# Queue order in the late attention heads: stores and loads first on SP, splits and output products behind the next head's scores and turns

## The chip, the cores and the metric

The program runs on one core of a Trainium2 chip. The metric is device time in microseconds (us). The engines are TensorE (matmuls; PE in the profile, its weight loads PEld), VectorE (DVE), ScalarE (ACT), GpSimd (POOL) and SyncE (SP), which here only issues transfers (DMAs). Each engine works through its own queue in order.

## The reference

For 4 × 8 = 32 heads of 576 positions and 64 columns, decayed causal attention; then two feed-forward layers over the 2304 tokens:

```
cum    = cumsum(log(clip(f, 1e-4, 1)))
scores = q k^T / 8 + cum[i] - cum[j], masked above the diagonal
attn   = exp(scores - max) / (sum + 1e-9);  o = attn v
x      = o, heads side by side: 2304 x 512
x      = relu(x w_in)^2 w_out            # first layer, 512 -> 2048 -> 512
h      = x w_in';  out = (h - tanh(h)) w_out'   # second layer, same sizes
```

## The kernel before, in words

Matmuls run on float32r operands; a product of full precision is made of three, with each operand split into a rounded part and the rest (`rounded` and `rest`, lines 93 to 106 by engine). So nearly each tile has a rounding and a subtraction behind it.

The main loop at the end of the function walks over feed-forward blocks: 8 of the first layer (288 tokens each), then 5 of the second. A block has 16 steps; step i issues 12 matmuls of the first product (`h_step`, line 143), and, two steps later, 12 of the second (`y_step`, line 169). Between these half steps the attention is advanced by pieces (`advance`): a generator `chain` gives one piece at each `yield`. Tokens 0 to 575 belong to heads 0 to 7 and so on, so blocks wait for x from the attention; x goes through DRAM (`store_x`, `load_x`).

Heads 0 to 15 turn the probabilities by TensorE. Heads 16 to 31 (`UT` = 16 on), the late ones, do it through DRAM, and the change is about them. For a late head k the steps are:

- `load(k)` (lines 228 to 232): q and k into R (one buffer), and decay rows into QB (two buffers); `load_v(k)` (line 250) into VR (two buffers). All transfers are issued by SP.
- `prep(k)`: R is rounded to QA on ScalarE; VectorE makes QA's rest, GpSimd QB's rounding (line 95) and QB's rest (line 106).
- `scores(k, t)` for tiles t = 4, 3, 2, 1, 0 of query rows, 576, 448, 320, 192 and 64 keys wide: two matmuls (lines 490, 491), a row minimum on VectorE (451) into the P tile T, the exponential on ScalarE (456), and a normalisation (465) by VectorE for t = 4, 2, 0 and by GpSimd for t = 3 and 1. The P tiles are two, used in turn.
- `turn(k, t)`: VectorE transposes the 32 × 32 blocks in place (517).
- `put_get(k)`: five stores of T to DRAM (526, 527: the "put") and six loads that bring it back rearranged (532, 534: the "get").
- `split_p(k, a)`, a = 0 for chunks 0 and 1, a = 1 for 2 and 3: per chunk a rounding on GpSimd into PTh (95) and a rest on VectorE into PTl (106). PTh and PTl have one buffer each.
- `prep_v(k)`: V rounded on ScalarE, its rest on GpSimd; `pv(k)` (570 to 576): the output products of PTh, PTl and V, and the copies into xs; every second head `store_x`.

In `attention_late` the body for k scores head k and finishes head k − 1, in five pieces. The order that is written is not the order of issue. The program is built twice: up to the start of block 2 (`MARK`) the written order is forced on each engine; after it a planner at build time issues, by its own estimate of when inputs are there, the earliest written of the instructions that are ready. `tc.issue_after(x)` adds, for each instruction of the block on x's engine, that it is queued behind x, without a wait for x to finish; `latest(engine)` is the last instruction written so far on that engine. Feed-forward steps carry such ties to earlier attention pieces (`SLK`).

Of the kernel before, what the change touches and what calls it, by code (L numbers as in the profile page):

```python
# [18 lines left out]
NU = B * H  # L19
# [14 lines left out]
UT = 16  # L34
# [24 lines left out]
def kernel(  # L59
# [25 lines left out]
    def pre(u):  # L85
        return "" if u < UT else "l_"

    def by(name):
        return {"A": nc.scalar, "V": nc.vector, "P": nc.gpsimd, "S": nc.sync}[ENG[name]]

    def rounded(eng, out, in_):
        if eng is nc.scalar:
            eng.activation(out, in_, AF.Copy)  # L93
        elif eng is nc.gpsimd:
            eng.tensor_scalar(out, in_, 1.0, 1.0, ALU.mult, ALU.mult)  # L95
        else:
            eng.tensor_copy(out, in_)
# [7 lines left out]
    def rest(eng, out, in_, hi):  # L105
        eng.tensor_tensor(out, in_, hi.bitcast(F32), ALU.subtract)  # L106
# [76 lines left out]
    def latest(engine):  # L183
        return next(x for x in reversed(nc.cur_bb.bb.instructions) if x.engine == engine)
# [43 lines left out]
    def load(u):  # L228
        R[u] = one.tile([128, 2, S], F32, tag="R", name="R")
        nc.sync.dma_start(R[u], qk[u])  # L230
        QB[u] = two.tile([68, 2, S], F32R, tag="QB", name="QB")
        nc.sync.dma_start(QB[u][64:68].bitcast(F32), aug_d[u])
# [7 lines left out]
    def prep(u):  # L240
        r = R.pop(u)
        qa = two.tile([128, 2, S], F32R, tag="QA", name="QA")
        QA[u] = qa
        split_qk(r, qa, QB[u], *(pre(u) + x for x in ("qb_q", "qa_lo", "qb_lo")))
        ST[u] = two.tile([128, 4, 6], F32, tag="ST", name="ST")
        by(pre(u) + "st").memset(ST[u], 1.0)

    def load_v(u):
        VR[u] = two.tile([128, 5, D], F32, tag="VR", bufs=2, name="VR")
        nc.sync.dma_start(VR[u], v[u])  # L250
# [216 lines left out]
    def bank(u, name):  # L467
        return psa.tile([128, 512], F32, tag="at", name=name)

    def blocks(u):  # L470
        return PT[u % 2].rearrange("p (k s j) -> p k s j", s=4, j=32)
# [3 lines left out]
    def prob(u, t, a, b):  # L475
        rows = 64 if t == 0 else 128
        if u < UT:
            return P[t][:rows, a:b]
        k0, sl = (16, 2) if t == 0 else (0, t - 1)
        return blocks(u)[:rows, k0 + a // 32:k0 + b // 32, sl]  # L480
# [34 lines left out]
    def turn(u, t):  # L515
        x = prob(u, t, 0, NKEY[t])
        nc.vector.transpose(x, x)  # L517
# [5 lines left out]
    def put_get(u):  # L523
        T, (d, e) = PT[u % 2], p_d[u % 2]
        for q in range(4):
            by("put").dma_start(d.rearrange("(i q) n -> q i n", q=4)[q], T[32 * q:32 * q + 32, :2048])  # L526
        by("put").dma_start(e, T[:, 2048:])
        src = d.rearrange("(i q) (a b n) -> b i (q a) n", q=4, a=4, b=4)
        end = e.rearrange("(q i) (b s n) -> b i q s n", q=4, b=2, s=2)
        for b in range(4):  # L530
            dst = T[32 * b:32 * b + 32]
            by("get").dma_start(dst[:, :2048].rearrange("p (q n) -> p q n", q=16), src[b])  # L532
            if b < 2:
                by("get").dma_start(dst[:, 2048:].rearrange("p (q n) -> p q n", q=4), end[b][:, :, 1])  # L534

    def split_p(u, a):
        src = PT[u % 2][:, :2048].rearrange("p (q a s j) -> p q a s j", q=4, a=4, s=4)
        for c in (2 * a, 2 * a + 1):
            s0 = max(0, c - 1)
            hi, lo = (late_pt(k)[:, :, CHUNK_AT[c]:CHUNK_AT[c] + 4 - s0] for k in "hl")  # L540
            rounded(by("pth"), hi, src[:, :, c, s0:])
            rest(by(f"ptl{c}"), lo, src[:, :, c, s0:], hi)

    def late_pt(k):
        return PT[k].rearrange("p c j -> p (c j)")[:, :1664].rearrange("p (q c j) -> p q c j", q=4, j=32)

    def pv(u):
        vh, vr = VH.pop(u), VR.pop(u)
        b, h = divmod(u, H)
        e = h % 2  # L550
        ps = bank(u, "o_ps")
        if u < UT:
            hi, lo = (PT[k] for k in "hl")
            po = ps.rearrange("p (s j) -> p s j", s=4)
            at = lambda p, c, t: p[:, 10 - 4 * c + t:14 - 4 * c]
            po4, p4 = ps[0:64, 384:512].rearrange("p (q j) -> p q j", q=4), blocks(0)[0:64, 12:16, 1]
            po_at = lambda t: po[:, t:]
            p0 = blocks(0)[0:64, 8:10, 0]
        else:
            hi, lo = (late_pt(k) for k in "hl")  # L560
            po = ps.rearrange("p (q s j) -> p q s j", q=4, s=4)
            at = lambda p, c, t: p[:, :, CHUNK_AT[c]:CHUNK_AT[c] + 4 - t]
            end = PT[u % 2][0:64, 2048:].rearrange("p (q s j) -> p q s j", q=4, s=2)
            po4, p4 = po[0:64, :, 3], end[:, :, 1]
            po_at = lambda t: po[:, :, t:]
            p0 = end[:, 0:2, 0]
        seq = [(hi, 0), (None, 4), (None, 0), (hi, 1), (lo, 1), (hi, 2), (lo, 2), (hi, 3), (lo, 3), (lo, 0)]
        for n, (pt, c) in enumerate(seq):
            if c == 4:
                nc.tensor.matmul(po4, vr[0:64, 4], p4, start=False, stop=False)  # L570
            elif pt is None:
                ps0 = bank(u, "o0_ps")
                nc.tensor.matmul(ps0[0:64, 0:64], vr[0:64, 0], p0, start=True, stop=True)
            else:
                t = max(0, c - 1)
                nc.tensor.matmul(po_at(t), vh[:, c].rearrange("p a d -> p (a d)"), at(pt, c, t), start=(n == 0), stop=(n == 9))  # L576
        if e == 0:
            XS[0] = two.tile([128, S], F32, tag="xs", name="xs")
        xs = XS[0]
        r = slice(64 * e, 64 * e + 64)  # L580
        xt = one.tile([64, 512], F32, tag="xsh", name="xt")
        rounded(nc.scalar, xt, ps[64:128])
        if u < UT:
            nc.vector.tensor_tensor(xs[r, 64:], ps[0:64], xt, ALU.add)
        else:
            nc.vector.tensor_tensor(
                xs[r, 64:].rearrange("p (s q j) -> p q s j", s=4, q=4),
                ps[0:64].rearrange("p (q s j) -> p q s j", q=4, s=4),
                xt.rearrange("p (q s j) -> p q s j", q=4, s=4), ALU.add,
            )  # L590
        rounded(by(pre(u) + "xs0"), xs[r, 0:64], ps0[0:64, 0:64])
        if e == 1:
            store_x(b, h // 2, xs, 0, S)
# [11 lines left out]
    def attention(u0):  # L605
        for p in range(u0 - 2, UT):
            if u0 - 1 <= p:
                load_v(p + 1)
            for t in (1, 4, 3, 2):
                if p >= u0:  # L610
                    trans(p, t)
                    yield
                if u0 <= p + 1:
                    scores(p + 1, t)
                    if t == 1:
                        scores(p + 1, 0)
                    elif p + 1 == UT:
                        turn(UT, t)
                    yield
                if t == 4 and p + 2 < NU:  # L620
                    prep(p + 2)
                if t == 3 and p >= u0:
                    prep_v(p)
            if p + 3 < NU:
                load(p + 3)
            if p >= u0:
                pv(p)
            if p + 1 == UT:
                turn(UT, 1)
                turn(UT, 0)  # L630
                put_get(UT)
            if p >= u0:
                yield

    def attention_late():
        for k in range(UT + 1, NU + 1):
            now = k < NU
            if now:
                load_v(k)
                clear(k)  # L640
                scores(k, 4)
            yield
            if now:
                scores(k, 3)
                turn(k, 4)
            yield
            if k + 1 < NU:
                prep(k + 1)
            prep_v(k - 1)
            split_p(k - 1, 0)  # L650
            if now:
                scores(k, 2)
                turn(k, 3)
            yield
            if k + 2 < NU:
                load(k + 2)
            split_p(k - 1, 1)
            if now:
                scores(k, 1)
                scores(k, 0)  # L660
                turn(k, 2)
            yield
            if now:
                turn(k, 1)
                turn(k, 0)
                put_get(k)
            pv(k - 1)
            yield

    X = {0: [f1.tile([128, NK, TB], F32R, tag="xhl", bufs=4, name="xhl") for _ in range(2)]}  # L670
# [223 lines left out]
```

## Time and profile before

| | |
|---|---|
| median of 3 runs (lowest, highest) | 1102.18 us (1101.27, 1104.58) |
| profiled execution: its time, its span | 1104.67 us, 1102.8 us |
| TensorE busy over the span | 1032.4 us (94%) |
| VectorE, ScalarE, GpSimd busy | 585.9, 526.7, 255.0 us |
| chain that ended last | PE 51%, DMA 9%, DVE 4%, SP's queue 4% |
| transfers | 137.99 MB, mean 125 GB/s |

Busy time is summed over stages with different limits; idle time of an engine that is not the limit costs nothing. The late heads run from about 255 to 585 us. In a row "[7.45 <-POOL PTh L95]" says that the engine stood idle for 7.45 us before, and what ended it. The name of a tile stands without its buffer number, so heads are told apart by order: a head's stores (line 526) come once, the first of head 16's at 256.68 us.

### The profile page before, as it was taken

The page shows a single profiled execution, that of the slowest core. Times are in us where ns is not written, and L with a number is a line of the kernel's source. Part 1 is how long each engine was busy: PE and PEld are TensorE (multiplying, and loading weights), DVE is VectorE, ACT ScalarE, POOL GpSimd, SP SyncE. Part 2 cuts the span into 40 slices and gives each one's busy share as a digit, 9 for nine tenths or more (in the row PEclk, how much of TensorE's full clock was granted, in tenths as well). Part 3 has the DMA queues.
Part 4 walks back from the last instruction along what each step waited for, and adds up shares of the span by engine and source line. Part 5 has one row for each costly group of instructions (what it writes and reads, how often), then busy time and mean ns, then how long its engine had stood idle before and what let it go on. Part 6 is the DMA issues. An engine that isn't in the chain of part 4 may idle for free.

```text
span 1102.8 us, 17026 instructions
## 1 busy us (share of the span) xinstructions
PE 1032.4 (94%) x6048; PEld 909.0 (82%) x6048; DVE 585.9 (53%) x1550; ACT 526.7 (48%) x1221; POOL 255.0 (23%) x374
## 2 busy tenths in 40 slices
PE   4899999998989789989799999999999999999998
PEld 3576779887978688879789999888888888888898
DVE  5886777776677666957533545644222222222222
ACT  6977777764554454645435757532222222222222
POOL 4244455555345353533310000000000000000000
PEclk9989999998998898999899999999999999999999
DMA  7556643228766758766738149300300200110010
GB/s 243 193 148 196 183 154 121 79 79 234 213 172 181 208 146 257 222 145 176 197 84 328 53 143 345 133 1 1 115 1 1 88 27 1 39 39 1 1 39 20
DMA packets 95558, 137.99 MB, mean 125 GB/s; under 512 B 12048, under 2 KB 72016, under 8 KB 93424
## 3 DMA queue, kind: packets, MB, share of 16 engines
q1 hardware_dynamic: 95472, 136.89, 41.4%
q8 instruction: 48, 0.79, 0.3%
q14 instruction: 38, 0.31, 0.1%
HBM read 94.99 MB, written 41.88 MB: 124 GB/s over the span
## 4 chain that ended last, share of the span: by engine, by line
PE 51%; DMA 9%; DVE 4%; SPq 4%; POOL 1%; issue 1%; ACT 1%; POOLq 0%; ACTq 0%; DVEq 0%
PE yp L169 25%; PE hp L143 24%; DMA p_d<-T 4%; DMA T<-p_d 3%; DVE PTl L106 1%; SPq L532 1%; SPq L526 1%; PE o_ps L576 1%; SPq L534 1%; POOL PTh L95 1%; DMA xhl<-x_d 1%; DMA raw<-in_w_dram 1%; DVE T L517 1%; DVE gl L106 1%; DVE T L465 0%
## 5 line engine op out<-in xcount | busy, mean ns | idle before, releaser
L143 PE MATMUL hp<-xhl,w 128*128 128x288 f32 (+2 forms) x2496 | 457.5, 331 | 6.7 <-ACT tmp L153 4.0
L143 PEld LDWEIGHTS hp<-xhl,w 128*128 128x128 f32 x2496 | 394.6, 194 | 45.5 <-ACT tmp L153 5.2
L169 PE MATMUL yp<-ghl,w 128*128 128x512 f32 (+1 forms) x960 | 214.9, 373 | 0.0
L169 PE MATMUL yp<-gh,w 128*128 128x288 f32 x1024 | 199.3, 301 | 0.0
L169 PEld LDWEIGHTS yp<-ghl,w 128*128 128x128 f32 x960 | 167.8, 188 | 34.2
L169 PEld LDWEIGHTS yp<-gh,w 128*128 128x128 f32 x1024 | 161.6, 192 | 1.6 <-issue 0.4
L158 DVE TENSOR_TENSOR tmp<-hp,tmp 128x512 f32<-128x512 f32 (+1 forms) x80 | 51.0, 638 | 208.2 <-ACT tmp L157 208.1
L157 ACT ACTIVATE tmp<-hp 128x512 f32<-128x512 f32 (+1 forms) x80 | 44.5, 556 | 223.2 <-PE hp L143 223.1
L169 PE MATMUL yp<-gl,w 128*128 128x288 f32 x512 | 132.7, 303 | 4.6 <-DVE gl L106 3.7
L153 ACT ACTIVATE tmp<-hp 128x288 f32<-128x288 f32 x128 | 51.7, 405 | 123.3 <-PE hp L143 121.7
L456 ACT ACTIVATE T<-T,ST 128x320 f32<-128x320 f32 (+4 forms) x152 | 82.8, 546 | 45.8 <-DVE ST L451 39.4
L169 PEld LDWEIGHTS yp<-gl,w 128*128 128x128 f32 x512 | 91.0, 193 | 7.2 <-DVE gl L106 5.1
L106 DVE TENSOR_TENSOR gl<-tmp,gh 128x288 fp32r<-128x288 f32 x96 | 47.8, 499 | 64.5 <-ACT tmp L155 63.9
L106 DVE TENSOR_TENSOR PTl<-T,PTh 128x512 fp32r<-128x512 f32 (+1 forms) x64 | 53.0, 857 | 50.0 <-POOL PTh L95 49.0
L106 DVE TENSOR_TENSOR ghl<-tmp,ghl 128x512 fp32r<-128x512 f32 (+1 forms) x80 | 51.1, 639 | 49.1 <-ACT ghl L93 43.8
L451 DVE CUSTOM_DVE_ANT_0 T<-s_ps,mk 128x320 f32<-128x320 f32 (+3 forms) x152 | 61.8, 421 | 21.4 <-PE s_ps L491 13.2
L465 POOL TENSOR_SCALAR T<-T,ST 128x448 f32<-128x448 f32 (+4 forms) x80 | 52.4, 657 | 89.6 <-DVE ST L460 43.3
L93 ACT ACTIVATE ghl<-tmp 128x512 fp32r<-128x512 f32 (+1 forms) x80 | 47.2, 590 | 49.9 <-DVE tmp L158 49.8
L576 PE MATMUL o_ps<-PTh,VH 128*128 128x512 f32 (+1 forms) x96 | 40.4, 421 | 29.3 <-POOL PTh L95 25.4
L95 POOL TENSOR_SCALAR PTh<-T 128x512 fp32r<-128x512 f32 (+1 forms) x64 | 43.9, 710 | 73.3 <-DMA T<-p_d 72.8
L106 DVE TENSOR_TENSOR w<-wst,w 128x512 fp32r<-128x512 f32 x64 | 45.8, 722 | 25.8 <-ACT w L93 25.6
L154 ACT ACTIVATE gh<-tmp 128x288 fp32r<-128x288 f32 x128 | 56.6, 443 | 4.4 <-PE yp L169 1.3
(119 smaller groups left out, 1217.3 us busy)
## 6 DMA issues: line engine op xcount, KB each, us to landing
raw<-in_w_dram SPq DMA_DIRECT2D x64, 512.0 KB
p_d<-T SPq DMA_DIRECT2D x64, 256.0 KB
T<-p_d SPq DMA_DIRECT2D x64, 256.0 KB
R<-in_qk_dram SPq DMA_DIRECT2D x24, 576.0 KB
xhl<-y_d SPq DMA_DIRECT2D x16, 512.0 KB
xhl<-x_d SPq DMA_DIRECT2D x14, 576.0 KB
y_d<-yst SPq DMA_DIRECT2D x14, 576.0 KB
VR<-in_v_dram SPq DMA_DIRECT2D x32, 160.0 KB
```

The costliest lines, as they stand in the source:

```text
L93: eng.activation(out, in_, AF.Copy)
L95: eng.tensor_scalar(out, in_, 1.0, 1.0, ALU.mult, ALU.mult)
L106: eng.tensor_tensor(out, in_, hi.bitcast(F32), ALU.subtract)
L143: nc.tensor.matmul(ps, w[:, k * 128:(k + 1) * 128], xk, start=(jj == 0), stop=(jj == 11))
L153: nc.scalar.activation(tmp, ps, AF.Relu)
L154: nc.scalar.activation(gh, tmp, AF.Square)
L158: nc.vector.tensor_tensor(tmp, ps, tmp, ALU.subtract)
L169: nc.tensor.matmul(yp[m][:, :n], w[:, c], x, start=(i == 0 and j == 0), stop=(i == NF - 1 and j == 2))
L451: nc.vector.tensor_tensor_reduce(out, s_in, m_in, -0.125, 3.0e38 if mn is None else mn, ALU.add, ALU.min, accum_out=acc)
L456: nc.scalar.activation(p, p, AF.Exp, bias=mn, scale=-1.0, accum_out=st[:rows, 1, t:t + 1])
L465: by(n_by).tensor_scalar(p, p, st[:rows, 3, t:t + 1], 1.0, ALU.mult, ALU.mult)
L576: nc.tensor.matmul(po_at(t), vh[:, c].rearrange("p a d -> p (a d)"), at(pt, c, t), start=(n == 0), stop=(n == 9))
```

## The change

`split_p(k - 1, 0)` is written behind `scores(k, 2)` and `turn(k, 3)` and tied behind the latest instruction of VectorE and of GpSimd; `split_p(k - 1, 1)` behind the scores of tiles 1 and 0 and `turn(k, 2)` and tied behind VectorE's latest. `pv(k - 1)` is tied behind TensorE's latest. The loads of V for k + 1 and of q, k and decay for k + 2 move to the end of the body, behind `put_get(k)` and `pv(k - 1)`, tied behind SP's latest. For head 18 `load` moves in the same way from `attention`.

```diff
@@ attention
-            if p + 3 < NU:
+            if p + 3 < NU and p + 1 < UT:
                 load(p + 3)
...
                 put_get(UT)
+                loads(UT)
             if p >= u0:
                 yield
+
+    def loads(k):
+
+        with tc.issue_after(latest(EngineType.SP)):
+            if k + 1 < NU:
+                load_v(k + 1)
+            if k + 2 < NU:
+                load(k + 2)
@@ attention_late
             if now:
-                load_v(k)
                 clear(k)
                 scores(k, 4)
...
             prep_v(k - 1)
-            split_p(k - 1, 0)
             if now:
                 scores(k, 2)
                 turn(k, 3)
+            with tc.issue_after(latest(EngineType.DVE)), tc.issue_after(latest(EngineType.Pool)):
+                split_p(k - 1, 0)
             yield
-            if k + 2 < NU:
-                load(k + 2)
-            split_p(k - 1, 1)
             if now:
                 scores(k, 1)
                 scores(k, 0)
                 turn(k, 2)
+            with tc.issue_after(latest(EngineType.DVE)):
+                split_p(k - 1, 1)
             yield
             if now:
                 turn(k, 1)
                 turn(k, 0)
                 put_get(k)
-            pv(k - 1)
+            with tc.issue_after(latest(EngineType.PE)):
+                pv(k - 1)
+            loads(k)
             yield
```

## Rows read from the trace of the kernel before

**Rows 1.** Windows: us, busy PE, PEld, DVE, ACT, POOL; PE clock, DMA share, GB/s.

```profile
255.00:585.00 330.00, 290.09 (x1898) 274.41 (x1897) 212.13 (x632) 160.22 (x407) 128.49 (x173) 0.91 0.69 187
...
695.00:1102.00 407.00, 403.93 (x1945) 337.07 (x1943) 127.32 (x206) 109.33 (x193) 0.00 (x0) 1.00 0.08 29
```

**Rows 2.** Waits of TensorE, 255 to 600 us: total, times, longest.

```profile
PE o_ps L576 <- POOL PTh L95: 25.4, 8, 7.4
```

**Rows 3.** Timeline of TensorE: start, duration, engine, line, operation, tiles, [idle before].

```profile
359.76 0.28 PE L491 MATMUL s_ps<-QB 68*128 68x64 f32 x1
...
369.96 0.80 PE L576 MATMUL o_ps<-PTh,VH 128*128 128x512 f32 x1 [7.45 <-POOL PTh L95]
```

**Rows 4.** Timeline of SP's queue: start and duration of issue.

```profile
296.15 2.69 SPq L526 DMA_DIRECT2D p_d<-T  x4
...
354.78 3.44 SPq L526 DMA_DIRECT2D p_d<-T  x4
...
364.50 1.22 SPq L532 DMA_DIRECT2D T<-p_d  x2
...
376.86 2.82 SPq L526 DMA_DIRECT2D p_d<-T  x4
...
388.57 2.99 SPq L526 DMA_DIRECT2D p_d<-T  x4
...
392.40 1.31 SPq L230 DMA_DIRECT2D R<-in_qk_dram  x1
...
475.87 1.18 SPq L230 DMA_DIRECT2D R<-in_qk_dram  x1
...
555.01 3.38 SPq L526 DMA_DIRECT2D p_d<-T  x4
```

**Rows 5.** Chain that ended last, in order of time: start, duration, what.

```profile
364.50 3.78 DMA T<-p_d
...
398.32 5.14 DMA T<-p_d
...
451.69 3.56 DMA R<-in_qk_dram
...
462.13 8.95 DMA xhl<-x_d
```

**Rows 6.** Timeline of ScalarE, heads 24 (QA) and 22 (T).

```profile
360.12 1.18 ACT L93 ACTIVATE QA<-R 128x1152 fp32r<-128x1152 f32 x1
...
361.72 0.47 ACT L456 ACTIVATE T<-T,ST 128x192 f32<-128x192 f32 x1
```

**Rows 7.** Timeline of GpSimd.

```profile
291.44 2.31 POOL L95 TENSOR_SCALAR PTh<-T 128x512 fp32r<-128x512 f32 x4
...
369.29 2.91 POOL L95 TENSOR_SCALAR PTh<-T 128x512 fp32r<-128x512 f32 x4 [9.43 <-DMA T<-p_d]
372.18 0.66 POOL L95 TENSOR_SCALAR QB<-QA 64x576 fp32r<-64x576 f32 x1
372.81 1.70 POOL L106 TENSOR_TENSOR QB<-R,QA 64x576 fp32r<-64x576 f32 x1
...
375.10 0.69 POOL L465 TENSOR_SCALAR T<-T,ST 128x192 f32<-128x192 f32 x1
...
545.60 2.49 POOL L95 TENSOR_SCALAR PTh<-T 128x512 fp32r<-128x512 f32 x4 [0.52 <-DMA T<-p_d]
```

**Rows 8.** Timeline of VectorE.

```profile
369.94 1.09 DVE L106 TENSOR_TENSOR PTl<-T,PTh 128x512 fp32r<-128x512 f32 x1 [6.64 <-POOL PTh L95]
...
375.51 0.47 DVE L451 CUSTOM_DVE_ANT_0 T<-s_ps,mk 128x320 f32<-128x320 f32 x1
...
376.08 0.88 DVE L517 STREAM_TRANSPOSE T<-T 128x192 f32<-128x192 f32 x3
...
412.09 1.36 DVE L465 TENSOR_SCALAR T<-T,ST 128x320 f32<-128x320 f32 x1
...
422.06 0.39 DVE L465 TENSOR_SCALAR T<-T,ST 128x320 f32<-128x320 f32 x1
```

## The prediction

> **What bounds the kernel now.** I read the windows first, then who waits for whom, then the timelines of one pair of heads. From 255 to 585 us, where the sixteen late heads run, TensorE is busy 290.09 of 330.00 us at a mean granted clock of 0.91, so it stands idle for 39.9 us; from 695 us on it is busy 403.93 of 407.00 [rows 1]. The change touches only the first of these stretches. There 25.4 us of TensorE's waiting, in 8 pieces, is an output product that waits for the rounding on GpSimd [rows 2]. One piece: head 22's last score starts at 359.76, head 21's first output product at 369.96 after 7.45 us of nothing [rows 3].
>
> TensorE is not what sets the pace, since it waits. A loop of latencies does: scores, turns, store ("put"), load back ("get"), rounding and split of one head, and only then scores again in the same one of two P tiles. Head 18's store starts at 296.15 and head 31's at 555.01, thirteen steps later [rows 4]: 258.86 / 13 = 19.91 us a head, 39.8 us for two, which is one pass of the loop.
>
> Head 21 shows its parts. Its store starts at 354.78 [rows 4]; its last loads are issued at 364.50 and landed 3.78 later, at 368.28 [rows 5]: a round trip of 13.5 us. GpSimd rounds it from 369.29 after 9.43 us of idleness [rows 7], VectorE splits from 369.94 after 6.64 [rows 8].
>
> Both engines work in order, and there lies the loss. Head 22's exponential for tile 1 starts on ScalarE at 361.72 and lasts 0.47 [rows 6], so it is done at 362.19. Its normalisation runs on GpSimd at 375.10, because head 21's four roundings (2.91) and then the rounding and rest of QB for head 24 (0.66 and 1.70) stand ahead [rows 7]. Its turns run at 376.08 [rows 8], its store at 376.86 [rows 4], 22.1 us after head 21's. For head 23 the normalisation happened to stand ahead of head 22's rounding, and its store follows after 11.7 us, at 388.57 [rows 4]. In nine of the fourteen heads 18 to 31 the rounding of the head before stands ahead of the last normalisation; the first such rounding is at 291.44, the last at 545.60 [rows 7].
>
> A pass without such a block is head 21 to 23: 388.57 − 354.78 = 33.8 us. Against the mean of 39.8 that is 6.0 us; over the 6.5 passes of the thirteen steps 39 us. This is the most that the change can give, and about TensorE's idle time.
>
> **The change part by part.** The profiled execution took 1104.67 us, 1.87 of it around its span of 1102.8, and 2.49 above the median of the runs, 1102.18. I work out a difference and take it off the median.
>
> *Split behind turns.* Nothing is added or removed: per head four roundings, four rests and ten products are put behind other instructions of their engines. The first half (chunks 0 and 1) may no longer precede turn 3 on VectorE, the second not turn 2; on GpSimd the first half is tied only behind the rest of V. So the normalisation of tile 1 and the last two turns are not tied ahead of anything; the second half merely comes after the scores of tile 1 in the written order, so a planner that takes the earlier written of two ready instructions lets that normalisation pass. In head 22: two roundings (1.46), then the normalisation (0.69) ends at 369.29 + 1.46 + 0.69 = 371.44, and after the first two rests the turn gives a store at about 373, 4 us sooner. If all four roundings stay ahead, only head 24's QB is gone from the queue (its data now come later, below): the last turns then stand behind the four rests on VectorE, which end just ahead of the row minimum at 375.51 [rows 8], so the store comes at about 375.5, 1.4 us sooner. If the normalisation passes all four, the store comes at about 364, some 12 us sooner. I take 4, the middle case, because the tie on GpSimd is the weak one. A pass has one store, and 9 in 14 of the stores are blocked: 4 × 9/14 × 6.5 = 17 us less; bounds 6 and 39 (the 50 of the best case is more than there is).
>
> *The tie costs something.* The second half now waits for turn 2, and the P tile comes free later by one turn, 0.88 / 3 = 0.3 us [rows 8]: 0.3 × 6.5 = 2 us more; bounds 0 and 4 (two turns). Hidden elsewhere it is not, since the tile's release is in the loop.
>
> *VectorE beside GpSimd.* More normalisations on VectorE will run beside GpSimd's work. The row shows what that can cost: 320 columns took 1.36 us at 412.09, in front of which VectorE had been free, and 0.39 at 422.06 [rows 8]. About 1.0 us in 9 of 14 heads is up to 4 us; I take 1, since the roundings that used to stand beside the rests now stand beside turns. The Trainium skill, "SBUF — State Buffer", section "SBUF: two separate sides", says that the two engines lock one pair of ports for a whole instruction and the loser stands still. By that rule every such meeting would cost the whole of GpSimd's instruction, and the term would be the full 4; the two rows agree with the lock, but not every meeting in the trace is that dear.
>
> *Loads behind the round trip.* Loads of q and k (R, QB) and of V are now queued on SP behind the head's gets (and, for odd heads' outputs, behind the stores of x). Head 26's load of R at 392.40 stood between head 23's store at 388.57 and its gets [rows 4], whose last was issued at 398.32 and landed 5.14 later [rows 5]: a round trip of 14.9 against 13.5. Two of the fourteen heads had it so, the other with R at 475.87 [rows 4]. Each gives 1.4 us to one of the two interleaved chains of passes, half to the end: 2 × 1.4 / 2 = 1 us less; bounds 0 and 5 (if R just ahead of a store did the same in half of the heads, 7 × 1.4 / 2).
>
> The price is that R comes a head or more later. After head 21's gets are issued (364.50 + 1.22) head 23's R would be issued at about 366.5 and land after 3.56 us, as one did [rows 5], at 370.1, or that much after the gets' landing, at 371.8. ScalarE's rounding of q and k takes 1.18 [rows 6], GpSimd's two QB steps 2.36 behind the four roundings, which end at 372.2 [rows 7]: 374.6 to 375.4, then the score product. Head 23's first row minimum is at 375.51 now, held by the P tile [rows 8]. So the new path ends where the old one ends: I take 0. But nothing is left in reserve. A large transfer ahead of R takes 8.95 where x was loaded [rows 5]: the upper bound is 8.95 − 3.56 = 5.4 us a pass, 35 in all; below, 0.
>
> *Output products behind TensorE's latest.* Head 21's product already stood ten us behind the last score, with feed-forward matmuls between [rows 3]. I take 0; bounds −3 and +3 for one group of feed-forward matmuls to either side.
>
> *The start.* Head 18's loads go behind head 16's gets, beside the load of x for the next block: 0, bounds 0 and 3.
>
> Sum: −17 + 2 + 1 − 1 = −15 us: 1104.67 would become about 1090, and the median 1102.18 − 15 = 1087 us. TensorE's idle time should fall from 39.9 to about 25 us; matmuls at the lower clock behind each stall get fewer, but that is inside the loop's time and not counted again.
>
> **The rivals.** *Clean passes.* All normalisations get ahead; the loop runs at 33.8 a pass: 39 less, 1063 us. For: head 23 shows that it happens. Against: the ties don't reach the normalisation of tile 1.
>
> *No change.* The planner puts all four roundings ahead as now, and the 6 us that the lower bounds leave are eaten by the tie and the start: 1102, within 3. For: the last two turns, for which the store waits, are untied.
>
> *Slower: R becomes the last to release the scores.* Place: the first score of head k+2 behind QB, behind R, behind the gets on SP. Price: if R lands 5.4 us later than reckoned in five of the passes, +27, less the 15 gained: +12, 1114 us. It decides the sign once R's path is longer than the P tile's by 15 / 6.5 = 2.3 us a pass. For: no reserve, and DMA share 0.69 in this stretch [rows 1]. Against: a head's gets end before R starts, so usually little is in front of it.
>
> **How the numbers follow.** Forecast (1072 to 1097) 0.42, clean passes 0.14, no change 0.14, R late 0.30. The range that leaves 2 in 10 out reaches into both sides: 1062 to 1118. What a measurement can tell from no change is 0.3%, 3.3 us. Faster: 0.42 + 0.14 = 0.56; same 0.14; slower 0.30.
>
> **What would show it.** Right: in the timeline of GpSimd the normalisation of tile 1 stands ahead of at least the second two roundings; store to store falls to about 18.7 us a head; the waits of TensorE's output products for GpSimd fall from 25.4 to about 12. R's loads stand behind the gets on SP, and none between a store and its gets. Wrong: TensorE or VectorE wait for QB or for R's landing by more than 2.3 us a pass, then the R rival holds; or store to store stays near 19.9 with the order on GpSimd as it was, then nothing has been moved. If the stretch to 585 us shrinks but the later one grows, something I left out has moved, such as the weights' loads on SP.

## The result, and the profile after

The changed kernel takes 1115.32 us (median of 4 runs, 1112.29 to 1117.34) against 1103.21 for the kernel before in the same comparison (1101.27 to 1104.58): a ratio of 1.0109, with an interval of 1.0079 to 1.0139. It is 12 us slower, where I had forecast 15 us less. The profiled execution took 1114.67 us, its span is 1112.9, 10.1 longer than that of before.

The windows of the changed kernel (columns as in [rows 1]):

```profile
255.00:585.00 330.00, 285.44 (x1860) 272.08 (x1859) 202.81 (x626) 159.29 (x403) 121.13 (x170) 0.91 0.68 185
585.00:695.00 110.00, 107.02 (x783) 105.84 (x782) 53.74 (x105) 66.63 (x150) 4.13 (x5) 0.98 0.61 214
695.00:1112.00 417.00, 414.00 (x2021) 347.35 (x2019) 132.05 (x215) 115.84 (x207) 0.00 (x0) 1.00 0.10 36
```

TensorE did 38 matmuls fewer in the late heads' stretch than before [rows 1], and GpSimd is still busy with them after 585 us (4.13). What isn't done there stands behind it: the last stretch, in which TensorE is busy for 414.00 of 417.00 us, ends 10 us later.

The waits of the changed kernel, 255 to 620 us (total, times, longest):

```profile
POOL PTh L95 <- DMA T<-p_d: 112.8, 16, 13.6
...
ACT QA L93 <- DMA R<-in_qk_dram: 59.9, 13, 8.0
...
PE o_ps L576 <- POOL PTh L95: 21.2, 8, 3.8
...
DVE T L517 <- POOL T L465: 17.0, 11, 7.4
```

The wait that I had watched, an output product for the rounding, fell a little, from 25.4 [rows 2] to 21.2, where I had forecast 12. Others are new or grew: GpSimd waits 112.8 us for loads before its roundings (72.8 before), VectorE's turns 17.0 us for GpSimd's normalisation (1.7 before), and ScalarE 59.9 us for R, thirteen times (before, not once in this window).

SP's queue in the changed kernel (start and duration of issue): the stores of heads 18, 21, 22 and 31, and between two of them the loads of the end of the body.

```profile
292.67 2.69 SPq L526 DMA_DIRECT2D p_d<-T  x4
...
351.50 2.70 SPq L526 DMA_DIRECT2D p_d<-T  x4
...
361.64 1.21 SPq L532 DMA_DIRECT2D T<-p_d  x2
362.90 0.62 SPq L250 DMA_DIRECT2D VR<-in_v_dram  x1
363.61 0.38 SPq L230 DMA_DIRECT2D R<-in_qk_dram  x1
...
374.54 2.69 SPq L526 DMA_DIRECT2D p_d<-T  x4
...
574.96 2.69 SPq L526 DMA_DIRECT2D p_d<-T  x4
```

From head 18's store to head 31's it is now (574.96 − 292.67) / 13 = 21.71 us a head; before it was 19.91 [rows 4]. Head 23's short interval of 11.7 us, on which my forecast rested, has no counterpart: the thirteen intervals lie between 18.3 and 27.3 us. The last store comes 20 us later, the end 10: while the late heads wait, TensorE does feed-forward work in part of the time, and that work is then not left for the end.

Why each store follows the one before is in the chain that ended last, 362 to 376 us (start, duration, what), of head 21's gets and head 22's store:

```profile
362.23 4.17 DMA T<-p_d
...
367.21 1.46 POOL PTh L95 x3
368.67 0.63 POOL T L465
...
369.89 0.35 DVE T L465
370.24 1.20 DVE PTl L106 x2
371.44 0.57 DVE T L465
372.01 0.28 DVE T L517
...
372.32 1.66 DVE QA L106
...
374.00 0.52 DVE T L517
...
374.54 0.32 SPq L526
```

Head 21's store at 351.50, its gets landed at 366.40 (14.9 us), its four roundings, head 22's normalisations, two rests, turns, QA's rest, and head 22's store at 374.54, 8.1 us after the landing: 23.0 us, and the next interval is 21.8. Head 22's exponentials were long done; ScalarE's timeline has tile 1's here:

```profile
360.71 0.44 ACT L456 ACTIVATE T<-T,ST 128x192 f32<-128x192 f32 x1
```

And GpSimd's timeline shows what stood in front:

```profile
366.63 2.04 POOL L95 TENSOR_SCALAR PTh<-T 128x512 fp32r<-128x512 f32 x4 [11.12 <-DMA T<-p_d]
368.65 1.04 POOL L465 TENSOR_SCALAR T<-T,ST 128x448 f32<-128x448 f32 x2
```

GpSimd stood idle for 11.12 us before a rounding whose data were not there, with two normalisations (tiles 3 and 1) behind it whose data were: VectorE had made the last of their reciprocals by 361.95. VectorE stood idle with it, before its turn of tile 3, behind which its first two rests are tied:

```profile
369.32 0.65 DVE L517 STREAM_TRANSPOSE T<-T 128x448 f32<-128x448 f32 x1 [7.38 <-POOL T L465]
```

I counted from the order of issue on GpSimd, for heads 18 to 31, in how many of them the last normalisation (tile 1) stands ahead of all four roundings of the head before (I call such a head "free"). Before it is 5 of 14; in the changed kernel 0 of 14. The normalisation of tile 3 stands behind the first rounding in 10 heads, before in 4.

### The profile page after: what moved, and what is told of

Read it like the earlier page. It is cut to its first block, busy times and chain, and to the rows that moved or that the text cites. A ratio compares the mean times of both kernels' runs of the same rounds, so it can differ in the third digit from the quotient of the medians.

```text
span 1112.9 us, 16999 instructions
## 1 busy us (share of the span) xinstructions
PE 1035.0 (93%) x6048; PEld 913.7 (82%) x6048; DVE 581.1 (52%) x1550; ACT 527.6 (47%) x1221; POOL 247.6 (22%) x374
## 4 chain that ended last, share of the span: by engine, by line
PE 63%; DMA 15%; DVE 7%; SPq 6%; POOL 3%; ACT 3%; issue 3%; POOLq 0%; DVEq 0%; ACTq 0%
PE yp L169 28%; PE hp L143 27%; DMA p_d<-T 6%; DMA T<-p_d 4%; DMA raw<-in_w_dram 2%; SPq L532 2%; DVE PTl L106 2%; PE o_ps L372 2%; PE o_ps L576 2%; DMA R<-in_qk_dram 1%; SPq L534 1%; SPq L526 1%; POOL PTh L95 1%; DVE QA L106 1%; PE t_ps L502 1%
## 5 line engine op out<-in xcount | busy, mean ns | idle before, releaser
L169 PE MATMUL yp<-gh,w 128*128 128x288 f32 x1024 | 204.1, 304 | 1.3 <-ACT gh L154 1.3
L169 PEld LDWEIGHTS yp<-gh,w 128*128 128x128 f32 x1024 | 164.6, 195 | 3.3 <-ACT gh L154 1.9
L106 DVE TENSOR_TENSOR PTl<-T,PTh 128x512 fp32r<-128x512 f32 (+1 forms) x64 | 45.2, 736 | 41.0 <-POOL PTh L95 40.9
L93 ACT ACTIVATE QA<-R 128x1152 fp32r<-128x1152 f32 (+1 forms) x32 | 33.7, 1054 | 65.5 <-DMA R<-in_qk_dram 65.1
L576 PE MATMUL o_ps<-PTh,VH 128*128 128x512 f32 (+1 forms) x96 | 41.3, 430 | 25.2 <-POOL PTh L95 21.2
L95 POOL TENSOR_SCALAR PTh<-T 128x512 fp32r<-128x512 f32 (+1 forms) x64 | 36.7, 598 | 112.8 <-DMA T<-p_d 112.8
```

What stands on the lines that cost most here:

```text
L169: nc.tensor.matmul(yp[m][:, :n], w[:, c], x, start=(i == 0 and j == 0), stop=(i == NF - 1 and j == 2))
```

## The experiments

The theories changed on the way. The expectations of e1 to e4 weigh theory L (R comes late and sets the pace) against theory S (the tied rests make VectorE's turns wait for GpSimd); both took the tie of the products to cost nothing. From e5 on they test theory B, here called *order*: the time follows the place of the last normalisations and turns against the roundings and rests of the head before, on GpSimd and VectorE, whichever part of the change moves them. Its rivals are *loads* (R late) and *products* (the tie on TensorE). All ratios are against the kernel before on the same chip, whose medians were 1103.68 (e1 to e4), 1106.87 (e5 to e8) and 1105.69 us (e9 to e12). "Step" is from head 18's store to head 31's, by 13.

**The parts alone.** e1_loads has only the moved loads:

```diff
-            if p + 3 < NU:
+            if p + 3 < NU and p + 1 < UT:
                 load(p + 3)
...
-                load_v(k)
...
-            if k + 2 < NU:
-                load(k + 2)
...
             pv(k - 1)
+            loads(k)
```

> Only the loads are moved behind put_get and pv and tied behind SP's latest; splits and output products stand as before. Theory L (late loads: R of head k+2 starts only after head k's gets, so the scores of k+2 start late, and the loop through R sets the pace): slower by most of what the whole change costs, 1113 to 1125 us; ScalarE's QA waits for R's landing about 60 us in all; store to store about 21.5 us. Theory S (the ties of the splits: VectorE's first two rests queue behind turn 3, whose normalisation on GpSimd stands behind the roundings of the head before): 1100 to 1106 us, with QA waiting for R but TensorE not; store to store at most 20.2.

Measured: 1111.95 us, ratio 1.0071 (1.0048 to 1.0094); 4 heads free, step 21.09. ScalarE's wait for R is 50.9 us. This lies between what the two theories gave.

e2_split has only the halves of the split moved and tied:

```diff
-            split_p(k - 1, 0)
...
+            with tc.issue_after(latest(EngineType.DVE)), tc.issue_after(latest(EngineType.Pool)):
+                split_p(k - 1, 0)
...
+            with tc.issue_after(latest(EngineType.DVE)):
+                split_p(k - 1, 1)
```

> Only the two halves of the split are moved and tied; loads and output products stand as before. Theory L: faster than before, 1085 to 1100 us, as the prediction's term for the splits; the normalisation of tile 1 stands ahead of some roundings on GpSimd. Theory S: slower, 1110 us or more, VectorE's turns wait for normalisations of GpSimd as in the changed kernel (17 us in all there).

Measured: 1111.25 us, ratio 1.0066 (1.0041 to 1.0092); 2 heads free, step 20.54. The part that I priced at −17 + 2 + 1 costs 7.6, as theory S said.

e3_pv has only the tie of the products:

```diff
-            pv(k - 1)
+            with tc.issue_after(latest(EngineType.PE)):
+                pv(k - 1)
```

> Only the output products are tied behind TensorE's latest. Both theories and the prediction: no difference, 1100 to 1106 us. If it is 1110 or more, the tie on TensorE is the cause and both theories fall.

Measured: 1120.99 us, ratio 1.0162 (1.0126 to 1.0198); 1 head free, step 21.97. The part that I priced at nothing is the dearest alone, and by the expectation's own words theories L and S both fall. Nothing on GpSimd was edited, yet its order changed. Head 23's normalisation, ahead of the rounding before the change, is behind it here (GpSimd's timeline of e3):

```profile
389.40 0.62 POOL L95 TENSOR_SCALAR PTh<-T 128x512 fp32r<-128x512 f32 x1 [7.06 <-DMA T<-p_d]
...
391.13 1.89 POOL L95 TENSOR_SCALAR PTh<-T 128x512 fp32r<-128x512 f32 x3
...
396.98 0.76 POOL L465 TENSOR_SCALAR T<-T,ST 128x192 f32<-128x192 f32 x1 [0.54 <-DVE ST L460]
```

Its store is at 398.48 instead of 388.57 [rows 4].

e4_split_pv is the changed kernel with the loads where they were (the lines of e1 taken back).

> The changed kernel with its loads put back where they stood before (splits and output products tied). Theory L: the loss goes, 1085 to 1104 us, and store to store falls to 20 us or less. Theory S: the loss stays, 1110 to 1120 us, store to store near 21.7.

Measured: 1112.57 us, ratio 1.0069 (1.0044 to 1.0094); 1 head free, step 21.24. The loss stays, as theory S had it. In the changed kernel the loads cost 3 to 4 us by this, but the two intervals overlap (1.0069 here, 1.0109 there), so that is not told from nothing.

The parts alone are +8, +8 and +17 us, together +12: they don't add. Each takes from the same 5 free heads, of which 4, 2, 1 and 0 are left.

**The order made whole.** e5_behind_early is the kernel before with both halves of the split behind the whole of the next head, products untied, loads where they were:

```diff
-            split_p(k - 1, 0)
...
-            split_p(k - 1, 1)
...
                 put_get(k)
+            with tc.issue_after(latest(EngineType.DVE)), tc.issue_after(latest(EngineType.Pool)):
+                split_p(k - 1, 0)
+                split_p(k - 1, 1)
             pv(k - 1)
```

> Both halves of a head's split are written behind all turns and the store of the next head, and tied behind VectorE's last turn and GpSimd's last normalisation; loads and output products as before the change. Theory B (a head's store is late because its last normalisation and turns queue behind the roundings and rests of the head before, whichever part of the change moves them there): no store waits for the round trip before it, store to store 18.7 us or less, 1065 to 1095 us. Theory P (the output products, later by this, hold the P tile and TensorE instead): 1103 us or more, with waits of TensorE for the splits above 25 us.

Measured: 1064.35 us, ratio 0.9629 (0.9604 to 0.9654); 14 heads free, step 16.85. GpSimd's timeline of e5 in one head:

```profile
353.25 1.17 POOL L465 TENSOR_SCALAR T<-T,ST 128x448 f32<-128x448 f32 x1
...
355.88 0.62 POOL L465 TENSOR_SCALAR T<-T,ST 128x192 f32<-128x192 f32 x1
356.48 4.00 POOL L95 TENSOR_SCALAR PTh<-T 128x512 fp32r<-128x512 f32 x4
```

Both normalisations stand ahead, and the roundings start with no idle time in front. The time is just below the lower end that theory B gave. Its windows:

```profile
255.00:585.00 330.00, 316.16 (x2202) 304.95 (x2201) 233.70 (x670) 184.30 (x467) 128.25 (x173) 0.96 0.76 216
```

TensorE does 304 matmuls more in the same 330 us than before [rows 1] and is idle for 13.8 us instead of 39.9; the granted clock rises from 0.91 to 0.96. GpSimd's wait for loads before a rounding is 18.4 us in e5:

```profile
POOL PTh L95 <- DMA T<-p_d: 18.4, 6, 6.2
```

The whole gain is of two kinds, as the page of e5 shows:

```profile
PE 1015.5 (96%) x6048; PEld 896.8 (84%) x6048; DVE 589.4 (56%) x1550; ACT 525.5 (50%) x1221; POOL 254.0 (24%) x374
```

Its span is 1061.6 us, so TensorE is idle for 46.1 us instead of 70.4 (1102.8 − 1032.4): 24.3 us less. The other 16.9 us of the 41.2 are busy time: the same 6048 matmuls take 1015.5 us instead of 1032.4, at a mean granted clock of 0.988 over the span instead of 0.971. In the kernel before, TensorE went from 1.00 (2.4 GHz) to 0.50 (1.2 GHz) over the 7.45 us of idleness of [rows 3]; the four microseconds behind it (columns as in [rows 1]):

```profile
370.00:374.00 4.00, 4.00 (x14) 3.43 (x15) 3.94 (x8) 0.00 (x0) 4.00 (x5) 0.50 0.56 180
```

e10_dve_tie is e5 with one tie less:

```diff
-            with tc.issue_after(latest(EngineType.DVE)), tc.issue_after(latest(EngineType.Pool)):
+            with tc.issue_after(latest(EngineType.DVE)):
```

> e5_behind_early without the tie on GpSimd: the splits are written in the same place and tied on VectorE alone, so that on GpSimd the normalisation of tile 1 precedes the roundings of the head before in 3 of 14 heads and not in 14. Theory B: most of the gain is lost, 1095 to 1115 us, store to store 19.5 us or more. If the rests on VectorE are what holds the store: within 8 us of e5.

Measured: 1107.81 us, ratio 1.0021 (1.0000 to 1.0041); 3 heads free, step 20.24. The written order is that of e5; only GpSimd's tie is gone, and with it the order on GpSimd and the whole gain, as theory B said. VectorE's order goes with it: the turn of tile 1, which needs GpSimd's normalisation, stands behind rests of the head before in 7 of 14 heads (in e5 in none). So the place in the text is not what gains; the order in the queues is, and e10 does not tell the two queues apart.

e11_half_behind puts the first half where the change has it, tied on both engines, and the second half behind all turns; loads and output products are as before the change:

```diff
                 turn(k, 3)
+            with tc.issue_after(latest(EngineType.DVE)), tc.issue_after(latest(EngineType.Pool)):
+                split_p(k - 1, 0)
...
                 put_get(k)
+            with tc.issue_after(latest(EngineType.DVE)), tc.issue_after(latest(EngineType.Pool)):
+                split_p(k - 1, 1)
```

> Early loads; the first half of the split as in the change (tied behind turn 3 on VectorE), the second behind all turns: in 12 of 14 heads the normalisation of tile 1 stands behind the first two roundings of the head before and ahead of the second two, which the prediction took for the likely order. By the prediction's term (4 us for a blocked store): 1080 to 1095 us. Theory B in its strict form (one rounding in front makes the store wait for the whole round trip): 1100 us or more, store to store 19.5 or more.

Measured: 1113.82 us, ratio 1.0071 (1.0046 to 1.0095); step 20.02. This is the order that I had forecast for the change: in 12 of 14 heads the normalisation of tile 1 lies between the halves, in the other 2 it is free. It is 0.7% slower than before, where my term would give 1080 to 1095. GpSimd's timeline of e11:

```profile
364.81 1.44 POOL L95 TENSOR_SCALAR PTh<-T 128x512 fp32r<-128x512 f32 x2 [4.40 <-DMA T<-p_d]
...
372.46 0.48 POOL L465 TENSOR_SCALAR T<-T,ST 128x192 f32<-128x192 f32 x1 [3.05 <-DVE ST L460]
372.90 0.88 POOL L95 TENSOR_SCALAR PTh<-T 128x384 fp32r<-128x384 f32 x2
```

The normalisation runs ahead of the second half, but 7.6 us behind the first, and waits for a reciprocal on VectorE. VectorE's timeline of e11 shows what that one stood behind:

```profile
366.90 0.65 DVE L517 STREAM_TRANSPOSE T<-T 128x448 f32<-128x448 f32 x1 [1.13 <-POOL T L465]
367.47 2.49 DVE L106 TENSOR_TENSOR PTl<-T,PTh 128x512 fp32r<-128x512 f32 x2
...
372.07 0.27 DVE L460 RECIPROCAL ST<-ST 128x1 f32<-128x1 f32 x3
```

A turn that waits for GpSimd, two rests of the head before, and only then the reciprocals, though tile 1's exponential ran on ScalarE at 366.07. The store is at 373.68, some 9 us behind the landing that GpSimd had waited for, and the two roundings are 1.44 of them. Two roundings and two rests in front are enough to lose the gain of e5, from which this kernel differs in nothing else that was written. That the store then hangs on the landing, and not on the length of the roundings, is how I read these rows; no run lengthens or shortens the roundings alone.

**Where the normalisations run.** e7_after_nv and e8_before_nv move the normalisations of tiles 1 and 3 from GpSimd to VectorE, in the changed kernel and in the kernel before:

```diff
-    ... "l_n1": "P", ... "l_n3": "P", ...
+    ... "l_n1": "V", ... "l_n3": "V", ...
```

> The changed kernel with the late heads' normalisations of tiles 3 and 1 on VectorE and not on GpSimd. Theory B: VectorE's turns no longer wait for normalisations behind roundings, and turn 3, 2 and 1 of a head can pass the round trip of the head before: store to store 20 us or less, 1085 to 1106 us. If loads or output products are the cause, the time stays at 1112 to 1120 us.

Measured: 1108.98 us, ratio 1.0028 (1.0007 to 1.0048); step 21.31. This lies between the two ranges that were expected. It is 0.8% better than the changed kernel (1.0109, the intervals apart): VectorE's turn of tile 3 now stands ahead of the rests in all 14 heads (10 in the changed kernel), but the turn of tile 1 still stands behind some in all 14.

> The kernel before with the same move of the two normalisations to VectorE. Theory B: nine of fourteen stores lose GpSimd's part of the block, 1085 to 1100 us. If VectorE's rests in front of the turns are the block and not GpSimd's queue: 1100 to 1110 us.

Measured: 1110.26 us, ratio 1.0042 (1.0027 to 1.0058); step 19.67. GpSimd's roundings no longer have a normalisation behind them, and neither kernel gets near e5, against what theory B expected of GpSimd's queue alone. The block in the other queue is left. The waits of e8, 255 to 620 us:

```profile
PE o_ps L576 <- POOL PTh L95: 36.0, 10, 5.2
...
DVE PTl L106 <- POOL PTh L95: 37.4, 13, 6.8
```

VectorE stands 37.4 us before rests, in thirteen pieces (49.0 in twelve in the kernel before). Its timeline shows one of them, and three normalisations of the next head behind it:

```profile
309.29 1.09 DVE L106 TENSOR_TENSOR PTl<-T,PTh 128x512 fp32r<-128x512 f32 x1 [3.97 <-POOL PTh L95]
...
315.73 0.75 DVE L465 TENSOR_SCALAR T<-T,ST 128x320 f32<-128x320 f32 x3
```

By the order of issue on VectorE, the turn of tile 1 stands behind rests of the head before in 8 of 14 heads of e8 (9 in the kernel before). So GpSimd's queue alone is not the cause; the order is needed on both.

**Loads with the order held.** e6_behind is e5 with the moved loads of e1.

> The same as e5_behind_early, with the loads of the change (behind the gets on SP). Theory B alone: as e5 within 6 us. Theory L (the late R sets the pace by itself): 10 us or more above e5, and ScalarE's QA waits for R's landing 50 us or more.

Measured: 1097.34 us, ratio 0.9928 (0.9903 to 0.9952); 14 heads free, step 20.25, in which intervals of 13.5 to 19 us and of 23 to 27 alternate. So the late loads cost 33 us against e5, as theory L said for this run. SP's queue in e6, two stores and R between them:

```profile
384.10 3.28 SPq L526 DMA_DIRECT2D p_d<-T  x4
...
397.56 0.38 SPq L230 DMA_DIRECT2D R<-in_qk_dram  x1
...
410.04 2.70 SPq L526 DMA_DIRECT2D p_d<-T  x4
```

GpSimd in e6 waits 10.39 us for the rounding of that R, and head 24's normalisations of tiles 3 and 1 stand behind it:

```profile
404.00 1.23 POOL L95 TENSOR_SCALAR QB<-QA 64x576 fp32r<-64x576 f32 x1 [10.39 <-ACT QA L93]
405.21 1.41 POOL L106 TENSOR_TENSOR QB<-R,QA 64x576 fp32r<-64x576 f32 x1
406.61 1.38 POOL L465 TENSOR_SCALAR T<-T,ST 128x448 f32<-128x448 f32 x2
```

It is the same block with another instruction at its head.

e12_behind_vlate is e5 with only V's load moved to the end of the body:

```diff
-                load_v(k)
...
             pv(k - 1)
+            if k + 1 < NU:
+                with tc.issue_after(latest(EngineType.SP)):
+                    load_v(k + 1)
```

> e5_behind_early with only the load of V moved behind the store, the gets and the output products (R and QB early as before). If the loads' price in e6_behind (33 us) is R's late landing: within 5 us of e5, 1060 to 1070 us. If it is SP's queue, blocked by V's load that waits for the output products: 1075 us or more.

Measured: 1063.67 us, ratio 0.9616 (0.9580 to 0.9652); step 16.97. V's load is free, and with it the rival that V's load blocks SP's queue is out; the 33 us need the loads of q, k and decay.

**Products with the order held.** e9_behind_pv is e5 with the tie of e3.

> e5_behind_early (splits behind all turns, loads early) with the output products tied behind TensorE's latest, as in the change. If that tie by itself holds TensorE or the P tile, it costs here what it cost alone (17 us): 1078 to 1085 us. If it cost there only because the order on GpSimd fell out worse: within 5 us of e5, 1060 to 1070 us.

Measured: 1058.06 us, ratio 0.9571 (0.9540 to 0.9602), the best of all; 14 heads free, step 16.98. The windows of e9, and one line of its waits, 255 to 620 us:

```profile
255.00:585.00 330.00, 318.60 (x2246) 307.22 (x2245) 238.94 (x676) 188.09 (x475) 127.63 (x173) 0.97 0.76 216
```

```profile
PE o_ps L576 <- POOL PTh L95: 2.5, 1, 2.5
```

The tie that alone cost 17 us is worth about 6 here (0.9571 against 0.9629, the intervals just apart), a little more than the expectation allowed for. The products now stand behind the scores of the next head, and TensorE's wait for the rounding falls from 9.7 us in e5 to 2.5.

All kernels beside each other; "behind" is the number of heads with the normalisation of tile 3 behind the first rounding:

| kernel | ratio | free of 14 | behind | step, us |
|---|---|---|---|---|
| before | 1 | 5 | 4 | 19.91 |
| e3 products | 1.0162 | 1 | 6 | 21.97 |
| changed | 1.0109 | 0 | 10 | 21.71 |
| e1 loads | 1.0071 | 4 | 6 | 21.09 |
| e11 half behind | 1.0071 | 2 | 2 | 20.02 |
| e4 split, products | 1.0069 | 1 | 6 | 21.24 |
| e2 split | 1.0066 | 2 | 5 | 20.54 |
| e10 one tie | 1.0021 | 3 | 5 | 20.24 |
| e6 behind, loads | 0.9928 | 14 | 0 | 20.25 |
| e5 behind | 0.9629 | 14 | 0 | 16.85 |
| e12 behind, V late | 0.9616 | 14 | 0 | 16.97 |
| e9 behind, products | 0.9571 | 14 | 0 | 16.98 |

## Why the prediction was wrong, point by point

**What bounds the kernel: right.** A loop of latencies set the pace, and an in-order queue blocked by a rounding set the loop's length. e5 takes the block away: the step falls to 16.85, as in the clean pass that I had read from heads 21 to 23 (33.8 us for two), and its 1064 us is what the clean-passes rival forecast (1063). That the time agrees so well is partly luck. I turned steps into time one for one, and left the clock out as counted already; in e5 24.3 us come from TensorE's idle time and 16.9 from shorter busy time. Nor does the step give the time elsewhere: e6 has a longer step than the kernel before (20.25 against 19.91) and is 0.7% faster, and the changed kernel's last store comes 20 us later, its end 10.

**Split behind turns, −17: this step failed, in sign.** I said that the tie on GpSimd is weak, and took the middle of three cases, that the normalisation would land between the halves and give 4 us a store. It landed there in 0 of 14 heads. The bounds were wrong too, in two ways. First, even the middle case is worth nothing: I shortened the store's delay by the two roundings and a QB behind the landing, but a store that must wait for the landing of the head before ties store to store to a whole round trip, and the rests on VectorE come in front of the reciprocals besides. e11 has that order in 12 heads and a step of 20.02. I could have seen the second point in the kernel before. I gave GpSimd's queue as the reason for head 22's normalisation at 375.10 [rows 7], but it needs a reciprocal too, and VectorE made the last two of that head only behind all four rests:

```profile
374.72 0.21 DVE L460 RECIPROCAL ST<-ST 128x1 f32<-128x1 f32 x2
```

Eight of the nine blocked heads of the kernel before have this order, so with VectorE's order as it was, room on GpSimd alone would not have helped them. Second, I took the five free heads for granted: my lower bound kept the order on GpSimd as it was. The change lost all five, and put tile 3's normalisation behind the roundings as well, so that VectorE's rests, tied behind turn 3, made a chain of both engines.

**The tie's cost, +2, and VectorE beside GpSimd, +1.** Not seen apart from the order. No run tells these two sizes.

**Loads: −1 and R late 0.** The gain is not seen. ScalarE waited for R thirteen times, as the rival said, though in the changed kernel e4 gives it only some 3 us of the 12, presumably because the store is late already. Alone (e1) the moved loads cost 8, with the order on GpSimd somewhat worse beside them, and with the blocks gone 33 us (e6), close to the upper bound of 35. My argument that the new path ends where the old one ends was made at the pace of the kernel before; at the pace of e5, R is what the next scores wait for.

**Products, 0 within 3: failed alone (+17), through the order on GpSimd.** I weighed the tie by the matmuls on either side. Its price lay in other engines' queues, whose order changed with it: where ties hold that order (e9), the same tie costs nothing.

**The start, 0: not contradicted.** Head 18's store came at 292.67, before the change at 296.15 [rows 4].

**The signs.** I wrote that a wrong result would show as TensorE or VectorE waiting for R, or as a step near 19.9 with the order as it was. The step is 21.71 and the order is worse: the case of a changed, worse order was missing among my cases. The late-R rival stood at 1114, near the measured time, but by e4 most of the measured loss is not its mechanism. So it is luck that the rival's figure and my range (1062 to 1118) reached the measured time.

**What stays open.** Why the planner put the normalisations behind in each of the kernels is not shown, only that it did, and that ties which fix the order on both engines bring the time down. The counts are not a scale: e1 keeps 4 free heads and still has a step of 21.09, with R late beside it, and e3 and e4 have the same two counts, 1 and 6, and are 8 us apart. So the loss of the changed kernel is put down to the order by its rows and by what e5, e10 and e11 do; how much of the 12 us each blocked head costs is not shown.

## What to carry to other kernels

In an in-order queue, an instruction that waits for a round trip through DRAM belongs behind all instructions of the next item that its store needs, on each engine that handles both items; with half of it in front, nothing was gained here. With a planner, look at the order that comes out for every queue: a tie on one engine can reorder another, so a part that costs nothing where it is written may be the dearest of all. When the pace has risen, test again any loads that were moved later: cover that was there at the old pace can be gone.

## What the runs showed of the hardware

The same four roundings on GpSimd took 2.04 us in the changed kernel, with VectorE idle beside them, and 4.00 us in e5, with VectorE at work. VectorE's timeline of e5 has in those 4 us, among others:

```profile
356.13 1.67 DVE L465 TENSOR_SCALAR T<-T,ST 64x64 f32<-64x64 f32 x1
...
358.51 1.71 DVE L106 TENSOR_TENSOR PTl<-T,PTh 128x512 fp32r<-128x512 f32 x3
```

A normalisation of 64 × 64 took 1.67 us there. Two heads later in e5 it took 0.25 us, with GpSimd idle when it began:

```profile
390.06 0.25 DVE L465 TENSOR_SCALAR T<-T,ST 64x64 f32<-64x64 f32 x1
```

So work on either engine goes with longer instructions on the other. The Trainium skill, "SBUF — State Buffer", section "SBUF: two separate sides", gives a reason: a shared pair of ports, which one of the two holds for a whole instruction while the other stands still. The rows agree with that, but show no lock as such. I had given this a term in the prediction (+1); e5 is 4% faster with the dearer meeting. TensorE then sets the pace, as it is busy for 316.16 of 330.00 us, and the meetings are covered.
